# One explicit issue order for the set-up, two batches and the third attention of a fused attention and gated-MLP kernel

## The chip, the cores and the metric

The kernel runs on one core of a Trainium2 chip. Such a core has five engines, each with an instruction queue of its own: TensorE (PE in the rows; PEld is its weight load), VectorE (DVE), ScalarE (ACT), GpSimd (POOL) and SyncE (SP), which here only issues DMAs. They meet at semaphores. The metric is the device time of one execution in microseconds; lower is better.

## The reference, cut to what matters

Eight batches of 576 tokens with 512 channels (8 heads of 64). Packed attention: 32 pack queries per head attend over the keys and values, and the tokens then attend over the 32 packed rows. A gated convolution and a spatial gating MLP follow.

```python
p_packed = sm_attn(p, k, v)                 # softmax(scale * p k^T) v
x = sm_attn(q, p_packed, p_packed)          # heads side by side: 576 x 512
gate = sigmoid(sum_k conv_w[k] * shifted(x, k))     # 5 taps, causal
x = (gate * (x @ w_val)) @ w_out
h = relu(x @ w_in);  u, v = halves(h)
v_n = (v - mean(v)) / sqrt(var(v) + 1e-6)
out = (u * (w_spatial @ v_n + b_spatial)) @ w_out2
```

The weight matrices arrive as float64; the rest is float32.

## The kernel before, in words

**Precision.** Most products are made from a high and a low half of each operand, both in the `fp32r` type: `split` copies to the high half on ScalarE and subtracts on VectorE for the low half; `mm3` issues three matmuls for each product.

**Set-up.** A float64 block is turned into float32 by `from_f64` (a "unit"): one ScalarE activation (L460), three VectorE instructions (L464, L467, L468) and an addition (L471), on VectorE for the five blocks in `DADD` and on GpSimd for the rest. Units `uo`, `uw`, `uv`, `uu` are four blocks each of w_out, the v half of w_in, w_val and the u half of w_in; `wo` does the same with w_out2, then splits. Units `uu` and `wo` share one temporary buffer ("late"), the others have four. `fold` (`fv`, `fu`) multiplies w_out into w_in, and its result is split into `wp` (L506, L507). `spatial` (`ws`) loads and splits the spatial weights. `cw`, `cb`, `cx` make the first batch's gates by another way (convolution taps folded into the packed rows), with sigmoids on L299.

**A batch.** Attention of the next batch: `sa` (scores, row maxima, exponentials), `tr`, `av`, `ppt`, `sb` and `sb2` (second softmax), `m`, then `xt` (output transposed, in two halves; the second is followed by four channel convolutions, L307 to L314: a ScalarE copy into `acc`, four accumulating VectorE steps, a ScalarE sigmoid into `gate`). MLP of this batch: `val` (four tiles of 12 matmuls, multiplied by the gates on L337 and split into `g`), `hv` (five row tiles, normalised into `vn`), `hu`, `sp`, and `out` (four tiles of 24 matmuls, evacuated on L447, one output DMA each). A token's digit names the tile, head group or half.

**What sets the order.** `START` (set-up and first attention), `FIRST` (first batch's MLP with the rest of the set-up and the second attention) and `LOOP` (each later batch) are lists of tokens; `run` traces each token whole. A scheduler that works with a time model of its own then places the instructions of all tokens on the engines' queues and gives out the buffers; so a token's instructions are interleaved with those of its neighbours. Matmul results go through four PSUM buffers of two banks (pool `ps2`); `f` has eight buffers, `g` four, `kq` three.

Of the kernel before, what the change touches and what calls it, by code (L numbers as in the profile page):

```python
# [16 lines left out]
P = 128  # L17
UGB = 5
DADD = ('u2', 'o0', 'o1', 'w1', 'w0')
START = """  # L20
ik0 ip0 ro0 ic0 ik1 sa0 iv1 uo0 iv0 rw0 tr0 lv0 rv0 ro1 uo1 cw0 rv1 cb0 lk0 lq0 rw1 uw0 tr1 uo3 uw1 av0 uw2 uo2 uv0 av1 uv1 uw3 lq1 fv3 fv0 fv1 lk1 ppt0 sb0 sb20 sb21 fv2 uv3 uv2 lp0 m0 cx0 cx1 lv1
"""
FIRST = """
val1 ru1 val0 val3 ru0 lv0 val2 sa0 uu2 uu0 hv0 uu1 tr0 ws3 tr1 uu3 fu2 fu0 ws4 hv3 wo0 lv1 ws1 hv2 av0 av1 fu1 lq0 fu3 ppt0 lq1 wo1 hv1 hv4 ws0 sb0 hu1 hu2 ws2 sb20 lp0 hu3 sb21 hu0 wo3 lk0 lk1 sp0 sp2 sp1 wo2 sp3 m0 xt0 out1 xt1 out3 out0 out2
# [7 lines left out]
def packed_attention_gated_mlp(  # L32
# [72 lines left out]
    def load_kq(kind, b, g):  # L105
        src = kT if kind == "k" else qT
        t = kq_p.tile([P, 2, S], F32, tag="kq", name="kq")
        nc.sync.dma_start(out=t, in_=src[b, g])
        kq_t[kind, b, g] = t

    def load_v(b, g):
        t = v_p.tile([P, 4, 5, 65], F32, tag="v", name="v")
        nc.sync.dma_start(out=t, in_=vT[b, g])
        v_t[b, g] = t

    def load_p(b):
        t = sm_p.tile([P, NC * NPK], F32, tag="pbd", name="pbd")
        nc.sync.dma_start(out=t, in_=pT[b])
        pbd_t[b] = t

    class Attn:
        def __init__(self, b):
            self.b = b
            self.a, self.aT = {}, {}
            self.sT, self.A, self.an = {}, {}, {}
            self.gate = {}

# [8 lines left out]
        def sa(self, _):  # L136
            ps, heads = self.heads(pbd_t.pop(self.b), "k")
            for i in range(0, 8, 2):
                for qt in range(4):
                    for g, h, pT_, k in heads[i:i + 2]:  # L140
# [4 lines left out]
                        )  # L145
            mx = sm_p.tile([P, 8], F32, tag="mx", name="mx")
# [13 lines left out]
            for g in range(2):  # L160
                a = f_p.tile([P, S], F32, tag="f", name="a")
# [8 lines left out]
        def tr(self, g):  # L170
            aT = sm_p.tile([P, NB, NPK], F32, tag="aT", name="aT")
            nc.vector.transpose(out=aT.rearrange("p a b -> p (a b)"), in_=self.a.pop(g))
            self.aT[g] = aT

        def av(self, g):
# [12 lines left out]
            if g == 0:  # L188
# [13 lines left out]
        def ppt(self, _):  # L202
            ps = ps2.tile([P, 2, 512], F32, tag="ps2", name="ps2")[:, 0, :P]
            nc.tensor.transpose(ps, self.pp.rearrange("p a b -> p (a b)"), ident)
            self.ppT = pp_p.tile([P, P], F32, tag="ppT", name="ppT")
            nc.scalar.copy(out=self.ppT, in_=ps)

        def sb(self, _):
# [8 lines left out]
            for g in range(2):  # L217
                self.softmax_n(g, ps[g])

        def softmax_n(self, g, ps):  # L220
# [8 lines left out]
            )  # L229
            nc.scalar.activation(out=sTf, in_=sTf, func=AF.Exp, scale=scale)  # L230
            self.sT[g] = sT

        def sb2(self, g):
# [9 lines left out]
            nc.vector.transpose(out=an, in_=sT.rearrange("p a b -> p (a b)"))  # L243
            hi = am_p.tile([P, S], F32R, tag="Ah", name="Ah")
            lo = am_p.tile([P, S], F32R, tag="Al", name="Al")
            split(hi, lo, an)
            self.A[g] = (hi, lo)
            self.an[g] = an

        def m(self, _):  # L250
            ps = ps2.tile([P, 2, 512], F32, tag="ps2", name="ps2")
            for h in range(4):
                hs = slice(NPK * h, NPK * h + NPK)
                for g in range(2):
# [4 lines left out]
                    )  # L259
            hi = am_p.tile([P, 2, DM], F32R, tag="Mh", name="Mh", bufs=1)  # L260
            lo = am_p.tile([P, 2, DM], F32R, tag="Ml", name="Ml", bufs=1)
            split(hi, lo, ps)
            self.M = (hi, lo)

        def xt(self, n):
# [9 lines left out]
            if n == 0:  # L275
# [3 lines left out]
            if n == 1:  # L279
                for c in range(4):  # L280
                    self.conv(c, self.x[c // 2][:, c % 2, :])

        def cx(self, n):
            ps = [ps2.tile([P, 2, 512], F32, tag="ps2", name="ps2") for _ in range(2)]
            for tap in reversed(range(CONV)):
                sft = CONV - 1 - tap
                lo = sft if n == 0 else 0
                for h in range(4):
                    hs = slice(NPK * h, NPK * h + NPK)
                    for g in range(2):  # L290
# [12 lines left out]
        def conv(self, c, x):  # L303
# [3 lines left out]
            nc.scalar.activation(out=acc, in_=x, func=AF.Copy, scale=cw[:, c, CONV - 1:CONV])  # L307
            for tap in range(CONV - 1):
# [4 lines left out]
                )  # L313
            nc.scalar.activation(out=gt, in_=acc, func=AF.Sigmoid)  # L314

    class Mlp:
# [6 lines left out]
        def val(self, c):  # L323
# [3 lines left out]
            for n in range(2):  # L327
# [7 lines left out]
                )  # L335
            t = f_p.tile([P, S], F32, tag="f", name="g1")
            nc.vector.tensor_tensor(  # L337
                out=halves(t), in0=ps[:, :, :SH], in1=halves(at.gate.pop(c)), op=ALU.mult
            )
            g = g_p.tile([P, 2, S], F32R, tag="g", name="g")  # L340
            split(g[:, 0, :], g[:, 1, :], t)
            if not self.g1:
                self.tail = vr_p.tile([P, NC, P], F32R, tag="tail", name="tail", bufs=1)
            nc.vector.tensor_copy(
                self.tail[:, c, :].rearrange("p (a b) -> p a b", a=2), f32(g)[:, :, S - 64:]
            )
            self.g1[c] = g

        def hv(self, tt):
# [25 lines left out]
            nc.vector.tensor_scalar_add(rstd[:w], mv[:w, 1:2], 1e-6)  # L375
            nc.gpsimd.tensor_tensor(out=rstd[:w], in0=rstd[:w], in1=mhalf[:w], op=ALU.pow)  # L376
            nc.vector.tensor_scalar(  # L377
                out=vr[:w], in0=vr[:w], scalar1=mv[:w, 0:1], scalar2=rstd[:w],
                op0=ALU.subtract, op1=ALU.mult,
            )  # L380
            if tt < NT - 1:
                split(vn[0][:, tt, :], vn[1][:, tt, :], vr)
            else:
                split(vn[0][:64, tt, :], vn[0][64:, tt, :], vr[:w])
                nc.scalar.copy(out=vn[1][:64, tt, :], in_=vr[:w])

        def hu(self, c):
            ps = ps2.tile([P, 2, 512], F32, tag="ps2", name="ps2")
            cs = slice(P * c, P * c + P)
            for n in range(2):  # L390
# [10 lines left out]
                )  # L401
            u = ug_p.tile([P, S], F32, tag="ug", name="u")
            nc.scalar.activation(out=halves(u), in_=ps[:, :, :SH], func=AF.Relu)
            self.u[c] = u

        def sp(self, c):
            ps = ps2.tile([P, 2, 512], F32, tag="ps2", name="ps2")
            cs = slice(P * c, P * c + P)
            for n in range(2):
# [12 lines left out]
                )  # L422
            t = f_p.tile([P, S], F32, tag="f", name="g2")
            nc.vector.tensor_tensor(  # L424
                out=halves(t), in0=ps[:, :, :SH], in1=halves(self.u.pop(c)), op=ALU.mult
            )
            g = g_p.tile([P, 2, S], F32R, tag="g", name="g")
            split(g[:, 0, :], g[:, 1, :], t)
            self.g2[c] = g

        def out(self, e):
            ps = ps2.tile([P, 2, 512], F32, tag="ps2", name="ps2")
            cs = slice(P * e, P * e + P)
            for n in range(2):
# [21 lines left out]
    def from_f64(dst, raw, n, pool, tag, last=nc.gpsimd):  # L456
# [5 lines left out]
        )  # L462
        ci, ei = c.bitcast(I32), e.bitcast(I32)
# [6 lines left out]
        )  # L470
        last.tensor_tensor(out=dst, in0=dst, in1=c, op=ALU.add)  # L471

    def raw64(slot, srcs):
        n = len(srcs)
        raw = (vn_p if slot == "vn1" else const).tile([P, n, 512, 2], I32, tag=slot, name="raw")
        for i, src in enumerate(srcs):
            nc.sync.dma_start(out=raw[:, i], in_=words(src))
        return [raw[:, i] for i in range(n)]
# [5 lines left out]
    def load_raw(name, slot, w, lo):  # L484
        k0 = int(name[-1]) * 2
        got = raw64(slot, [w[:, k, lo:lo + DM] for k in (k0, k0 + 1)])
        for i in range(2):
            raws[name[:-1], k0 + i] = got[i]

    def unit(kind, k, dst, temps):  # L490
        from_f64(dst, raws.pop((kind, k)), DM, *temps, nc.vector if kind + str(k) in DADD else nc.gpsimd)
# [7 lines left out]
    def fold(m, hf):  # L499
# [4 lines left out]
        mms(ps, [(woT[k][:, cs], win[k]) for k in range(NC)])  # L504
        hi, lo = wp[0][:, m, hs], wp[1][:, m, hs]
        nc.scalar.copy(out=hi, in_=ps)  # L506
        nc.vector.tensor_tensor(out=lo, in0=ps, in1=f32(hi), op=ALU.subtract)  # L507

    def spatial(t):
        if not ws:  # L510
            ws[:] = [const.tile([P, NT, S], F32R, tag=f"ws{i}", name=f"ws{i}") for i in range(2)]
        st = f_p.tile([P, S], F32, tag="f", name="stage")
        if t < NT - 1:
            nc.sync.dma_start(out=st, in_=wsT[:, t, :])
            split(ws[0][:, t, :], ws[1][:, t, :], st)
            return
        nc.sync.dma_start(out=st, in_=wsT[:, t, :])
        nc.scalar.copy(out=ws[0][:, t, :], in_=st)
        st = f_p.tile([P, S], F32, tag="f", name="stage")
        nc.sync.dma_start(out=st[:97], in_=wsT[:97, t + 1, :])  # L520
        w = ws[1][:, t, :]
        nc.scalar.copy(out=w[64:96], in_=st[64:96])
        hi = f_p.tile([P, S], F32R, tag="f", name="hi")
        for r in (slice(0, 64), slice(96, 97)):
            split(hi[r], w[r], st[r])

    def final(k):
# [10 lines left out]
    def tap_rows():  # L538
# [6 lines left out]
        )  # L545
        ps = ps2.tile([P, 2, 512], F32, tag="ps2", name="ps2")
        nc.tensor.transpose(ps[:n, 1, P:2 * P], cw.rearrange("p a b -> p (a b)"), ident)
        t = sm_p.tile([n, P], F32, tag="cwt", name="cwt", bufs=1)
        nc.scalar.copy(out=t, in_=ps[:n, 1, P:2 * P])
        ps = ps2.tile([P, 2, 512], F32, tag="ps2", name="ps2").rearrange("p a b -> p (a b)")  # L550
        for k in range(CONV):
            nc.tensor.matmul(
                ps[:, P * k:P * k + P], lhsT=sel[:, k].rearrange("p a b -> p (a b)"), rhs=t, start=True, stop=True
            )
        r = x_p.tile([P, CONV, P], F32, tag="x", name="cwr")
        nc.scalar.copy(out=r.rearrange("p a b -> p (a b)"), in_=ps[:, :CONV * P])
        cwr.append(r)

    def run(order, b, at, ml):
        setup = {  # L560
# [113 lines left out]
```

## Time and profile before

| | us |
|---|---|
| three runs | 639.28, 638.68, 639.39 (median 639.28) |
| the profiled execution | 639.22 |
| its span, first to last instruction | 637.4 |
| PE busy in the span | 596.7 |
| DVE busy | 446.0 |
| ACT busy | 292.3 |
| POOL busy | 49.3 |

The span is one execution as the hardware profiler recorded it; 1.82 us of that execution lie outside it. Busy time is an average over a set-up and eight batches that are not alike, so the rows below go by stretch. A float32 matmul of an instruction list stands as two records in the trace, an `fp32r` one as one.

### The profile page before, as it was taken

To read this page: it belongs to the slowest core of one execution; us is meant where nothing else is said; L and a number is where in the kernel's file an instruction comes from. 1 tells how busy PE (TensorE), PEld (TensorE's weight loads), DVE (VectorE), ACT (ScalarE), POOL (GpSimd) and SP (SyncE) were. 2 spreads that over 40 slices of the span, in tenths; PEclk is the share of its full clock that TensorE was granted. 3 is DMA by queue.
4 is the path that set the end of the run, shared out by engine and by line. 5 is a ranking of instruction groups with operands and counts; after the bars stand their busy time and mean duration, and the time that the engine had idled before them with its cause. 6 is when DMAs were issued, how large, how long until landed. Compare 5 with 4: busy or idle time off the path is not lost.

```text
span 637.4 us, 12474 instructions
## 1 busy us (share of the span) xinstructions
PE 596.7 (94%) x5267; PEld 514.7 (81%) x5267; DVE 446.0 (70%) x873; ACT 292.3 (46%) x503; POOL 49.3 (8%) x67
## 2 busy tenths in 40 slices
PE   3687697999999999999999999999999999999997
PEld 2323663898988898899889888989889988989997
DVE  4998355977957696687759685869667875965640
ACT  2522435636463564346543655355533744363422
POOL 1242002200010000100010001000010001000100
PEclk9985797999999999999999999999999999999999
DMA  8960053302322012401222132202240110010001
GB/s 331 408 226 1 1 194 124 127 1 76 114 88 76 20 59 77 159 1 76 80 85 75 53 102 86 75 20 77 64 149 1 75 39 1 2 57 20 1 1 74
DMA packets 16569, 52.48 MB, mean 82 GB/s; under 512 B 1953, under 2 KB 2977, under 8 KB 16514
## 3 DMA queue, kind: packets, MB, share of 16 engines
q1 hardware_dynamic: 16514, 51.70, 22.7%
q8 instruction: 41, 0.67, 0.4%
q14 instruction: 14, 0.11, 0.1%
HBM read 42.25 MB, written 9.44 MB: 81 GB/s over the span
## 4 chain that ended last, share of the span: by engine, by line
PE 80%; DVE 9%; DMA 5%; ACT 3%; POOL 1%; issue 1%; SPq 0%; ACTq 0%; POOLq 0%
PE ps L95 72%; DMA raw<-w_outT 3%; DMA stage<-wsT 2%; PE ps L141 2%; DVE mx L148 2%; PE ps L271 1%; PE ps L181 1%; PE ps L212 1%; ACT L163 1%; DVE tmp L467 1%; PE ps L256 1%; ACT a L163 1%; DVE tmp L464 1%; DVE m L154 1%; POOL winu L471 1%
## 5 line engine op out<-in xcount | busy, mean ns | idle before, releaser
L95 PE MATMUL ps<-ws,vn 128*128 128x288 f32 (+1 forms) x896 | 124.0, 296 | 0.0
L95 PEld LDWEIGHTS ps<-ws,vn 128*128 128x128 f32 (+1 forms) x896 | 120.3, 188 | 2.9 <-issue 2.8
L95 PE MATMUL ps<-g,wp 128*128 128x288 f32 x768 | 113.6, 297 | 0.0
L95 PEld LDWEIGHTS ps<-g,wp 128*128 128x128 f32 x768 | 106.8, 188 | 4.4 <-DVE g L337 1.3
L95 PEld LDWEIGHTS ps<-g,wo 128*128 128x128 f32 x768 | 102.2, 188 | 6.1 <-issue 3.5
L95 PE MATMUL ps<-g,wo 128*128 128x288 f32 x768 | 105.6, 296 | 0.0
L95 PE MATMUL ps<-wp,g 128*128 128x512 f32 x384 | 98.7, 402 | 3.2 <-ACT a L163 3.2
L310 DVE SCALAR_TENSOR_TENSOR acc<-x,cw,acc 128x572 f32<-128x572 f32 (+3 forms) x112 | 82.6, 813 | 24.7 <-ACT acc L307 24.7
L95 PEld LDWEIGHTS ps<-wp,g 128*128 128x128 f32 x384 | 69.6, 188 | 22.1 <-ACT a L163 5.2
L90 ACT CAST g<-g 128x576 fp32r<-128x576 f32 x64 | 43.2, 674 | 73.7 <-DVE g L424 57.1
L376 POOL TENSOR_TENSOR rstd<-rstd,mhalf 128x1 f32<-128x1 f32 (+1 forms) x40 | 24.2, 606 | 460.7 <-DVE rstd L375 460.7
L91 DVE TENSOR_TENSOR g<-g,g 128x576 fp32r<-128x576 f32 x64 | 49.3, 772 | 11.0 <-ACT g L90 10.3
L371 DVE BATCH_NORM_STATS2 st<-vr 128x6 f32<-128x512 f32 (+1 forms) x40 | 27.5, 690 | 30.0 <-ACT vr L364 26.9
L95 PE MATMUL ps<-Ah,Mh 128*128 128x288 f32 x128 | 39.1, 305 | 5.1 <-ACT gate L299 5.1
L90 ACT CAST vn<-vr 128x512 fp32r<-128x512 f32 (+1 forms) x40 | 24.7, 618 | 33.5 <-DVE vr L377 33.5
L95 PE MATMUL ps<-Ah,Ml 128*128 128x288 f32 x128 | 39.0, 305 | 0.0
L95 PE MATMUL ps<-Al,Mh 128*128 128x288 f32 x128 | 39.0, 304 | 0.0
L424 DVE TENSOR_TENSOR g<-ps,u 128x576 f32<-128x576 f32 x32 | 24.1, 754 | 19.1 <-PE ps L95 19.0
L377 DVE TENSOR_SCALAR vr<-vr,mv,rstd 128x512 f32<-128x512 f32 (+1 forms) x40 | 21.5, 538 | 22.5 <-POOL rstd L376 22.4
L447 ACT COPY o<-ps 128x576 f32<-128x576 f32 x32 | 20.3, 635 | 34.8 <-PE ps L95 34.8
L91 DVE TENSOR_TENSOR vn<-vr,vn 128x512 fp32r<-128x512 f32 (+1 forms) x40 | 27.1, 680 | 11.4 <-ACT vn L90 11.3
L364 ACT ACTIVATE vr<-ps 128x512 f32<-128x512 f32 x32 | 19.5, 611 | 30.2 <-PE ps L95 17.4
(111 smaller groups left out, 735.8 us busy)
## 6 DMA issues: line engine op xcount, KB each, us to landing
v<-vT SPq DMA_DIRECT2D x16, 650.0 KB, 5.1
kq<-kT SPq DMA_DIRECT2D x16, 576.0 KB, 4.3
kq<-qT SPq DMA_DIRECT2D x16, 576.0 KB, 4.8
outT<-o SPq DMA_DIRECT2D x32, 288.0 KB, 2.1
raw<-w_in SPq DMA_DIRECT2D x8, 512.0 KB, 10.6
raw<-w_outT SPq DMA_DIRECT2D x4, 512.0 KB, 8.7
raw<-w_val SPq DMA_DIRECT2D x4, 512.0 KB, 9.4
raw<-w_out SPq DMA_DIRECT2D x4, 512.0 KB, 5.2
```

The lines of the kernel that those rows point to most:

```text
L90: nc.scalar.copy(out=hi, in_=src)
L91: nc.vector.tensor_tensor(out=lo, in0=src, in1=f32(hi), op=ALU.subtract)
L95: nc.tensor.matmul(out, lhsT=a, rhs=b, start=(i == 0), stop=(i == len(pairs) - 1))
L141: nc.tensor.matmul(ps[g][NPK * qt:NPK * qt + NPK, h // 2, SQ * (h % 2):SQ * (h % 2) + SQ], lhsT=pT_, rhs=k[:, SQ * qt:SQ * qt + SQ], start ...
L148: nc.vector.tensor_reduce(mx[:, 4 * g:4 * g + 4].rearrange("p (a b) -> p a b", a=2), ps[g][:, :, :SH].rearrange("p a (b c) -> p a b c", b= ...
L310: nc.vector.scalar_tensor_tensor(out=acc[:, sft:], in0=x[:, :S - sft], scalar=cw[:, c, tap:tap + 1], in1=acc[:, sft:], op0=ALU.mult, op1=A ...
L364: nc.scalar.activation(out=vr, in_=ps, func=AF.Relu)
L371: nc.vector.bn_stats(st[:w], vr[:w])
L376: nc.gpsimd.tensor_tensor(out=rstd[:w], in0=rstd[:w], in1=mhalf[:w], op=ALU.pow)
L377: nc.vector.tensor_scalar(out=vr[:w], in0=vr[:w], scalar1=mv[:w, 0:1], scalar2=rstd[:w], op0=ALU.subtract, op1=ALU.mult,)
L424: nc.vector.tensor_tensor(out=halves(t), in0=ps[:, :, :SH], in1=halves(self.u.pop(c)), op=ALU.mult)
L447: nc.scalar.copy(out=halves(t), in_=ps[:, :, :SH])
```

## The change

The token methods become generators with a `yield` between pieces: after the matmuls, between the ScalarE and the VectorE part of a split, before a DMA, and so on. `START` and `FIRST` and the first pass through `LOOP` are replaced by `HEAD`, a list of about 500 pieces: `tok` runs a token to its end, `tok.n` runs n of its pieces, and a leading digit is the batch. `HEAD` is traced inside `manual_schedule`, so that every engine gets its instructions in the order of the list. Batches 2 to 7 are traced with `LOOP` as before, by the scheduler. The instructions are the same ones on the same engines; two more loads of ScalarE's table are among them (18 in place of 16).

```diff
-START = """
-FIRST = """
+HEAD = """
+ro0.1 ip0 cb0.1 ro0 ik0 ik1 ro1 0ws3.1 ic0 uo0.1 lk0 uo0.1 rw0.1 uo1.1 iv1 uo0 uo1.1 iv0 sa0.1 uo1 rv0.1 uo2.1 sa0.1
...
+1xt1.2 1out3.1 1xt1.1 1out3 1xt1
 """
...
     def split(hi, lo, src):
         nc.scalar.copy(out=hi, in_=src)
+        yield
         nc.vector.tensor_tensor(out=lo, in0=src, in1=f32(hi), op=ALU.subtract)
...
             acc = f_p.tile([P, S], F32, tag="f", name="acc")
             nc.scalar.activation(out=acc, in_=x, func=AF.Copy, scale=cw[:, c, CONV - 1:CONV])
+            yield
             for tap in range(CONV - 1):
...
+            yield
             nc.scalar.activation(out=gt, in_=acc, func=AF.Sigmoid)
...
-    def run(order, b, at, ml):
...
+    def steps(b, name, i):
+        if name in setup:
+            return setup[name](i)
+        if name in load:
+            return load[name](b, i)
+        if hasattr(Mlp, name):
+            return getattr(mls[b], name)(i)
+        return getattr(ats[b + 1], name)(i) if b + 1 < B else ()
+
+    def run(order, batch):
+        live = {}
         for tok in order.split():
+            tok, _, n = tok.partition(".")
+            name = tok.lstrip("01")
+            b = batch if len(name) == len(tok) else int(tok[0])
+            if tok not in live:
+                live[tok] = steps(b, name[:-1], int(name[-1]))
+            for _ in itertools.islice(live[tok], int(n) if n else None):
+                pass
...
-    run(START, -1, at, None)
-    for b in range(B):
-        ml = Mlp(at)
-        at = Attn(b + 1) if b + 1 < B else None
-        run(FIRST if b == 0 else LOOP, b, at, ml)
+    with tc.manual_schedule():
+        run(HEAD, -1)
+    for b in range(2, B):
+        run(LOOP, b)
```

ScalarE's queue up to the first sigmoids, before. `raw_625` and `raw_584` are blocks of the u half of w_in, `raw_825` one of w_out2; `gate` is what the first batch's sigmoids write.

```order
L460 ACTIVATE tmp_715<-raw_625 128x512
L90 CAST Ah_428<-an_426 128x576
L460 ACTIVATE tmp_751<-raw_625 128x512
L460 ACTIVATE tmp_767<-raw_584 128x512
L460 ACTIVATE tmp_828<-raw_825 128x512
L299 ACT_TABLE_LOAD
L299 ACTIVATE gate_508<-ps2_466 128x288
```

The same place in the changed kernel. `raw_419` is a block of the u half of w_in, `Mh` the high half of the product that `val` multiplies with.

```order
L114 CAST Ah_466<-an_456 128x576
L342 ACT_TABLE_LOAD
L342 ACTIVATE gate_522<-ps2_471 128x288
L342 ACTIVATE gate_524<-ps2_471 128x288
L342 ACTIVATE gate_526<-ps2_472 128x288
L342 ACTIVATE gate_528<-ps2_472 128x288
L521 ACTIVATE tmp_545<-raw_419 128x512
L114 CAST Mh_589<-ps2_535 128x1024
```

Three unit activations moved from ahead of the first sigmoids to behind them, and the units of two blocks and of w_out2 behind `val`.

ScalarE's queue at the convolutions of the third batch's attention, before. `x` is the transposed attention output, two tiles of two channel groups; `acc` one group's accumulator; `o` an output tile of batch 1.

```order
L278 COPY x_2167<-ps2_2201 128x2x288
L307 ACTIVATE acc_2214<-x_2167,cw_103 128x576
L307 ACTIVATE acc_2222<-x_2167,cw_103 128x576
L278 COPY x_2168<-ps2_2202 128x2x288
L307 ACTIVATE acc_2230<-x_2168,cw_103 128x576
L307 ACTIVATE acc_2238<-x_2168,cw_103 128x576
L447 COPY o_2270<-ps2_2245 128x576
L447 COPY o_2298<-ps2_2273 128x576
L314 ACT_TABLE_LOAD
L314 ACTIVATE gate_2213<-acc_2214 128x576
L447 COPY o_2328<-ps2_2303 128x576
L314 ACTIVATE gate_2221<-acc_2222 128x576
```

The same place in the changed kernel.

```order
L319 COPY x_2168<-ps2_2258 128x2x288
L319 COPY x_2169<-ps2_2259 128x2x288
L350 ACTIVATE acc_2287<-x_2168,cw_103 128x576
L507 COPY o_2305<-ps2_2270 128x576
L359 ACT_TABLE_LOAD
L359 ACTIVATE gate_2286<-acc_2287 128x576
L350 ACTIVATE acc_2310<-x_2168,cw_103 128x576
L359 ACTIVATE gate_2309<-acc_2310 128x576
L350 ACTIVATE acc_2318<-x_2169,cw_103 128x576
L359 ACTIVATE gate_2317<-acc_2318 128x576
L350 ACTIVATE acc_2326<-x_2169,cw_103 128x576
```

Three of the four `acc` copies moved behind the sigmoid of the group before them.

TensorE's queue around the second half of `xt` (8 matmuls) of the same attention, before. The tile ahead of it is the first of batch 1's four `out` tiles; three more follow before the next batch's `val`.

```order
L95 MATMUL ps_2171<-g,wo_823 128x288 x2
L95 MATMUL ps_2171<-g,wo_824 128x288
L271 MATMUL ps_2201<-an,pp 64x288 x4
L271 MATMUL ps_2202<-an,pp 64x288 x4
L95 MATMUL ps_2245<-g,wo_823 128x288 x2
L95 MATMUL ps_2245<-g,wo_824 128x288
```

The same place in the changed kernel. The tile ahead of it is the third of the four `out` tiles; the tile behind it (`ps_2270`) is the last, and `val` follows at once.

```order
L120 MATMUL ps_2230<-g,wo_395 128x288 x2
L120 MATMUL ps_2230<-g,wo_396 128x288
L311 MATMUL ps_2258<-an,pp 64x288 x4
L311 MATMUL ps_2259<-an,pp 64x288 x4
L120 MATMUL ps_2270<-g,wo_395 128x288 x2
L120 MATMUL ps_2270<-g,wo_396 128x288
```

Two `out` tiles, 48 matmuls, moved from behind the second half of `xt` to ahead of it.

## Rows read from the trace of the kernel before

**Rows 1.** Page, busy tenths in 40 slices of the span; PEclk is the granted clock.

```profile
PE   3687697999999999999999999999999999999997
...
PEclk9985797999999999999999999999999999999999
```

**Rows 2.** Five stretches: busy us (instructions) by engine, granted clock, DMA share, GB/s.

```profile
0.00:70.26 70.26, 41.66 (x396) 19.89 (x396) 52.36 (x103) 23.76 (x45) 19.63 (x23) 0.87 0.57 219
70.26:118.19 47.93, 43.10 (x314) 29.56 (x314) 28.31 (x65) 21.94 (x45) 5.31 (x6) 0.87 0.31 106
118.19:220.45 102.26, 101.73 (x914) 92.69 (x914) 76.52 (x144) 49.25 (x82) 7.85 (x8) 1.00 0.22 75
220.45:245.50 25.05, 24.51 (x222) 22.89 (x221) 20.63 (x40) 14.93 (x25) 0.00 (x0) 1.00 0.28 97
245.50:637.40 391.90, 385.74 (x3425) 349.64 (x3425) 268.16 (x523) 182.44 (x309) 16.46 (x30) 1.00 0.16 56
```

**Rows 3.** Chain that ended last: start us, us, what.

```profile
66.23 1.27 POOL winu L471
...
67.53 0.66 ACT tmp L460
...
68.20 1.28 ACT L299
...
70.26 9.35 PE ps L95 x48
...
83.95 13.35 DMA stage<-wsT
...
117.03 1.16 PE ps L212 x32
...
216.41 3.37 PE ps L95 x24
...
239.78 1.42 DVE mx L148 x2
```

**Rows 4.** DVE in order of time: start, us, line, op, tiles [idle before, releaser].

```profile
12.44 1.42 DVE L148 TENSOR_REDUCE mx<-ps 128x4 f32<-128x576 f32 x2
...
24.49 0.69 DVE L471 TENSOR_TENSOR winv<-winv,tmp 128x512 f32<-128x512 f32 x1
...
29.75 1.37 DVE L467 TENSOR_SCALAR tmp<-tmp 128x512 int32<-128x512 int32 x1
...
37.40 0.75 DVE L226 TENSOR_REDUCE mx<-sT 128x18 f32<-128x576 f32 x1
38.19 0.76 DVE L227 TENSOR_TENSOR sT<-sT,mx 128x576 f32<-128x576 f32 x1
...
58.48 0.75 DVE L91 TENSOR_TENSOR Al<-an,Ah 128x576 fp32r<-128x576 f32 x1
...
61.55 0.43 DVE L467 TENSOR_SCALAR tmp<-tmp 128x512 int32<-128x512 int32 x1
...
221.98 11.00 DVE L310 SCALAR_TENSOR_TENSOR acc<-x,cw,acc 128x572 f32<-128x572 f32 x15 [3.58 <-ACT acc L307]
```

**Rows 5.** POOL in order of time, one addition of the set-up.

```profile
29.45 1.38 POOL L471 TENSOR_TENSOR woT<-woT,tmp 128x512 f32<-128x512 f32 x1 [0.96 <-DVE woT L468]
```

**Rows 6.** PE in order of time, first `val` matmul and the one wait behind it.

```profile
70.26 0.61 PE L95 MATMUL ps<-Ah,Mh 128*128 128x288 f32 x1 [5.05 <-ACT gate L299]
...
102.02 1.31 PE L181 MATMUL ps<-v,aT 128*32 128x65 f32 x40 [4.21 <-DVE wp L507]
```

**Rows 7.** ACT in order of time around the spatial weights and the convolutions.

```profile
97.37 0.67 ACT L522 CAST ws<-stage 32x576 fp32r<-32x576 f32 x1 [7.56 <-DMA stage<-wsT]
...
220.49 0.64 ACT L278 COPY x<-ps 128x576 f32<-128x576 f32 x1
221.17 1.45 ACT L307 ACTIVATE acc<-x,cw 128x576 f32<-128x576 f32 x2
...
229.37 0.69 ACT L314 ACTIVATE gate<-acc 128x576 f32<-128x576 f32 x1 [0.38 <-DVE acc L310]
```

More of the change, by code (lines that the diff above doesn't have):

```diff
@@ L1 @@
+import itertools
 from contextlib import ExitStack
@@ L119, in load_p @@
         pbd_t[b] = t
+        yield
     class Attn:
@@ L217, in sb @@
             for g in range(2):
-                self.softmax_n(g, ps[g])
+                yield
+                yield from self.softmax_n(g, ps[g])
         def softmax_n(self, g, ps):
@@ L243, in sb2 @@
             nc.vector.transpose(out=an, in_=sT.rearrange("p a b -> p (a b)"))
+            self.an[g] = an
+            yield
             hi = am_p.tile([P, S], F32R, tag="Ah", name="Ah")
             lo = am_p.tile([P, S], F32R, tag="Al", name="Al")
-            split(hi, lo, an)
             self.A[g] = (hi, lo)
-            self.an[g] = an
+            yield from split(hi, lo, an)
         def m(self, _):
@@ L259, in m @@
                     )
+            yield
             hi = am_p.tile([P, 2, DM], F32R, tag="Mh", name="Mh", bufs=1)
             lo = am_p.tile([P, 2, DM], F32R, tag="Ml", name="Ml", bufs=1)
-            split(hi, lo, ps)
             self.M = (hi, lo)
+            yield from split(hi, lo, ps)
         def xt(self, n):
@@ L280, in xt @@
                 for c in range(4):
-                    self.conv(c, self.x[c // 2][:, c % 2, :])
+                    yield
+                    yield from self.conv(c, self.x[c // 2][:, c % 2, :])
         def cx(self, n):
@@ L339, in val @@
             )
+            yield
             g = g_p.tile([P, 2, S], F32R, tag="g", name="g")
-            split(g[:, 0, :], g[:, 1, :], t)
             if not self.g1:
                 self.tail = vr_p.tile([P, NC, P], F32R, tag="tail", name="tail", bufs=1)
+            self.g1[c] = g
+            yield from split(g[:, 0, :], g[:, 1, :], t)
             nc.vector.tensor_copy(
@@ L380, in hv @@
             )
+            yield
             if tt < NT - 1:
-                split(vn[0][:, tt, :], vn[1][:, tt, :], vr)
+                yield from split(vn[0][:, tt, :], vn[1][:, tt, :], vr)
             else:
-                split(vn[0][:64, tt, :], vn[0][64:, tt, :], vr[:w])
+                yield from split(vn[0][:64, tt, :], vn[0][64:, tt, :], vr[:w])
+                yield
                 nc.scalar.copy(out=vn[1][:64, tt, :], in_=vr[:w])
@@ L426, in sp @@
             )
+            yield
             g = g_p.tile([P, 2, S], F32R, tag="g", name="g")
-            split(g[:, 0, :], g[:, 1, :], t)
             self.g2[c] = g
+            yield from split(g[:, 0, :], g[:, 1, :], t)
         def out(self, e):
@@ L470, in from_f64 @@
         )
+        yield
         last.tensor_tensor(out=dst, in0=dst, in1=c, op=ALU.add)
[L473 to L478, printed above, removed]
     woT, winv, winu = [], [], []
@@ L485, in load_raw @@
         k0 = int(name[-1]) * 2
-        got = raw64(slot, [w[:, k, lo:lo + DM] for k in (k0, k0 + 1)])
+        raw = (vn_p if slot == "vn1" else const).tile([P, 2, 512, 2], I32, tag=slot, name="raw")
         for i in range(2):
-            raws[name[:-1], k0 + i] = got[i]
+            if i:
+                yield
+            nc.sync.dma_start(out=raw[:, i], in_=words(w[:, k0 + i, lo:lo + DM]))
+            raws[name[:-1], k0 + i] = raw[:, i]
     def unit(kind, k, dst, temps):
-        from_f64(dst, raws.pop((kind, k)), DM, *temps, nc.vector if kind + str(k) in DADD else nc.gpsimd)
+        return from_f64(dst, raws.pop((kind, k)), DM, *temps, nc.vector if kind + str(k) in DADD else nc.gpsimd)
     def u_half(k):
@@ L503, in fold @@
         hs = slice(hf * DM, (hf + 1) * DM)
-        mms(ps, [(woT[k][:, cs], win[k]) for k in range(NC)])
+        for k in range(NC):
+            nc.tensor.matmul(ps, lhsT=woT[k][:, cs], rhs=win[k], start=(k == 0), stop=(k == NC - 1))
+            yield
         hi, lo = wp[0][:, m, hs], wp[1][:, m, hs]
         nc.scalar.copy(out=hi, in_=ps)
+        yield
         nc.vector.tensor_tensor(out=lo, in0=ps, in1=f32(hi), op=ALU.subtract)
@@ L512, in spatial @@
         st = f_p.tile([P, S], F32, tag="f", name="stage")
+        nc.sync.dma_start(out=st, in_=wsT[:, t, :])
+        yield
         if t < NT - 1:
-            nc.sync.dma_start(out=st, in_=wsT[:, t, :])
-            split(ws[0][:, t, :], ws[1][:, t, :], st)
+            yield from split(ws[0][:, t, :], ws[1][:, t, :], st)
             return
-        nc.sync.dma_start(out=st, in_=wsT[:, t, :])
         nc.scalar.copy(out=ws[0][:, t, :], in_=st)
+        yield
         st = f_p.tile([P, S], F32, tag="f", name="stage")
         nc.sync.dma_start(out=st[:97], in_=wsT[:97, t + 1, :])
+        yield
         w = ws[1][:, t, :]
@@ L524, in spatial @@
         for r in (slice(0, 64), slice(96, 97)):
-            split(hi[r], w[r], st[r])
+            yield from split(hi[r], w[r], st[r])
+            yield
     def final(k):
@@ L531, in final @@
         nc.sync.dma_start(out=raw, in_=words(w_out2[:, k, :]))
+        yield
         t = f_p.tile([P, S], F32, tag="f", name="stage")[:, :DM]
-        from_f64(t, raw, DM, *late)
-        split(wo2[0][:, k, :], wo2[1][:, k, :], t)
+        yield from from_f64(t, raw, DM, *late)
+        yield
+        yield from split(wo2[0][:, k, :], wo2[1][:, k, :], t)
     cwr = []
@@ L597, in packed_attention_gated_mlp, with load_cw @@
-    at = Attn(0)
+    def load_cw():
+        nc.sync.dma_start(out=cw64, in_=words(conv_w))
+        yield
+    ats = [Attn(b) for b in range(B)]
+    mls = [Mlp(at) for at in ats]
+    setup = {
+        "cw": lambda i: from_f64(cw.rearrange("p a b -> p (a b)"), cw64, NC * CONV, *early),
+        "cb": lambda i: tap_rows(),
+        "ro": lambda i: load_raw(f"o{i}", ("wo20", "ws1")[i], w_outT, 0),
+        "rw": lambda i: load_raw(f"w{i}", ("wo21", "vn1")[i], w_in, DM),
+        "rv": lambda i: load_raw(f"v{i}", ("wo20", "wo21")[i], w_val, 0),
+        "ru": lambda i: load_raw(f"u{i}", ("ws1", "wo20")[i], w_in, 0),
+        "uo": lambda k: unit("o", k, woT[k], early),
+        "uw": lambda k: unit("w", k, winv[k], early),
+        "uv": lambda k: unit("v", k, wval[:, k, :], early),
+        "uu": lambda k: unit("u", k, u_half(k), late),
+        "fv": lambda m: fold(m, 1),
+        "fu": lambda m: fold(m, 0),
+        "ws": spatial,
+        "wo": final,
+        "ip": load_p,
+        "ik": lambda i: load_kq("k", 0, i),
+        "iv": lambda i: load_v(0, i),
+        "ic": lambda i: load_cw(),
+    }
```

116 lines of the change are left out of this document (69 added, 47 removed).

## The prediction, made before the changed kernel ran

> **What bounds the kernel now.** I read the page's slices first: TensorE is at nine tenths from the eighth slice on, and below that, at a granted clock down to half, only before [rows 1]. So there are two regimes. The stretches say how much each holds [rows 2]: from 245.50 us to the end TensorE works 385.74 of 391.90 us; from 118.19 to 245.50 it lacks about 1 us. All the idle time worth having is ahead of 118.19 us: 70.26 - 41.66 = 28.60 us before the first `val`, 47.93 - 43.10 = 4.83 us between it and the first `hu`.
>
> Then the chain, to see what ends those waits. The first `val` starts at 70.26 us because ScalarE's sigmoids came late, and they came late because their queue held unit activations, each waiting for GpSimd to give back the one "late" buffer: POOL addition, activation, table load, sigmoid, matmul [rows 3]; the matmul had waited 5.05 us [rows 6]. Ahead of that VectorE works almost without a gap from the row maxima at 12.44 to the last low half `Al`, which ends at 59.23 us [rows 4]. So the set-up has two limits in series: some 46.8 us of VectorE, then 11.0 us of sigmoids kept back. Between `val` and `hu` it is a DMA of the spatial weights, 13.35 us on the chain [rows 3], for which ScalarE waited 7.56 us [rows 7]; TensorE felt 4.21 us of it [rows 6].
>
> I cut the execution at four marks on TensorE: V (first `val`, 70.26), H (first `hu`, 118.19), X (the third attention's second `xt` half done, 220.45) and Y (245.50, where TensorE resumes behind the next attention's exponentials). Behind Y the two versions have the same 2898 matmuls in the same order, so 391.90 us stay. The new value of each stretch follows.
>
> **V, 57.5 us.** The instructions that VectorE has in its queue from the row maxima to `Ml`, the last operand of `val`, are those of before up to `Al`, less one unit addition and one `wp` subtraction (0.6 us each at the pitch of the rows, durations 0.69 in [rows 4]) and with `cw` added (0.3): -0.9 us. A VectorE instruction that meets a GpSimd addition lasts longer: L467 took 1.37 us beside an addition of 1.38 us and 0.43 us alone [rows 4, 5], 0.94 us for each meeting. Before, seven such meetings lie ahead of 59 us; in the new order I count six, since transposes or PSUM reads follow some units. So 12.44 + 46.79 - 0.9 - 0.9 = 57.4, taken as 57.5. TensorE's four folds, two `cx` and `m` fit beside it. Of the moved unit activations one still waits for the late buffer, but ahead of `Ml` and not of the sigmoids of the first half. Bounds: no meeting costs anything (seven times 0.94 less: 51.7), or nothing is gained but the sigmoids' 11 us and some transposes wait too (61).
>
> The Trainium skill (SBUF — State Buffer, Who interferes with whom) says that VectorE and GpSimd share a pair of ports under an exclusive lock, and that a VectorE instruction with at most one SBUF input, outside the fast modes, doesn't take it. The 1.37 us agree with the lock; no row here shows a transpose beside a GpSimd addition. By the rule the transposes put behind units hide an addition each; without it V would be about 2 us later.
>
> **V to H, 43.6 us.** Work stays: 43.10 us, less `sb` (1.16) [rows 3], which now follows H: 41.9. The spatial weights are loaded before 50 us and split late, so the 4.83 us of idle time go. In their place I see two short waits: the third block of the u half of w_in is finished only as the first `fu` fold wants it, and `hu` waits for the split of the last fold (ScalarE 0.6, VectorE 0.7). I put 1.7 us; 0 to 8 are possible, since VectorE now has some 36 us of work in these 43, by a count of its queue at the durations before.
>
> **H to X, 111.4 us.** Before 102.26. The 0.53 us idle go, `sb` comes in (1.16), and two `out` tiles of 24 matmuls move ahead of X: 2 x 3.37 = 6.74 [rows 3]. That is 109.6. Walking the queues I find short waits only (`hv` for the last `g`, a PSUM buffer behind a ScalarE copy): 1.8 us, 0 to 5. On SP the load of a key tile waits from about 138 us for `sb` of the third attention at about 185, and batch 0's output DMAs stand behind it; the buffers that they hold are wanted again only after that, so I put nothing.
>
> **X to Y, 31.0 us.** Here the cost is. Before, four `acc` copies were made at once and VectorE ran 15 convolution steps in 11.00 us, alternating groups, 0.73 us each [rows 4, 7]. Now each group's copy stands on ScalarE behind the sigmoid of the group before, so the two engines take turns. The four steps of a group also depend on each other, and a VectorE instruction that depends on the one before starts only after its whole duration (0.75 us long, next one 0.79 later [rows 4]), so a group takes about 4 x 0.85 = 3.4 us. From X: two `x` copies and `acc` (0.64, 0.61, 0.75) to 2.1; three rounds of 3.4 + sigmoid 0.69 + copy 0.75 to 16.4; meanwhile the first three `val` products; the fourth group between splits of `g` to 22.5; its sigmoid, product, split to 25.2; then from the maxima to TensorE's release, 245.50 - 239.78 = 5.72 [rows 3]: 30.9, with a gap or two 31.0. TensorE reaches `val` 6.74 us earlier than before, so it only waits longer: it has 18.3 us of work in 31.0. Bounds: not under 25.05 (the same VectorE work as before), not over 34.
>
> The Trainium skill (ScalarE: Activation LUTs, What ACT_TABLE_LOAD costs) gives 2.66 us for each change of table, with a drain behind the load. The trace disagrees: the load of 1.28 us at 68.20 is followed by a sigmoid at 69.50 [rows 3]. By the rule the load in this chain would end 1.4 us later and Y with it; by the trace it is inside the sum.
>
> **Sum.** 57.5 + 43.6 + 111.4 + 31.0 + 391.9 = 635.4 us of span, against 637.4; with 1.82 us outside, 637.2 us, where the profiled execution took 639.22 and the median is 639.28. About 17 us are won ahead of the first `hu`, and 15 are given back: 9 between H and X and 6 behind X. The 6.74 us of `out` are not lost as work, but as cover: they no longer stand beside the convolutions.
>
> **Rivals.**
> *The convolutions run as tightly as before* (X to Y 25.05): 637.2 - 5.95 = 631.3 us. For it: the VectorE work is the same. Against: the queue order of ScalarE, in which a copy can't pass a sigmoid. It would need `val` to be late enough to hide the turns.
> *The set-up gains more.* The 48 matmuls of the first `val` took 9.35 us, 0.195 each, where `out` matmuls of the same shape took 3.37 / 24 = 0.14 [rows 3], behind TensorE's idle time and at a granted clock of 0.87 in that stretch [rows 2]; if the denser folds and `cx` leave the clock higher, some 2.6 us go, and with half of the meetings hidden, 3 us more: 631.6 us. Against: TensorE still waits before V.
> *Slower: VectorE becomes the bound between `val` and the folds.* Place: the first `hv` to the split of the last fold. `hv` tiles, the units of `wo` and `uu`, maxima and transposes stand in one fixed queue, and each normalisation waits for GpSimd. Four additions block for 0.94 us each, 3.8 us, and one wait for a load like that of before costs TensorE 4.2 [rows 6]: 8.0 us instead of 1.7, or 643.5 us. It decides from about 3.5 us of waits on. For it: 36 us of VectorE in 43. Against: TensorE has four PSUM buffers to run ahead with.
>
> **How the numbers follow.** Forecast 637.2 us, with its own range of 634 to 641: chance 0.46. Convolutions tight 0.2, set-up better 0.14, VectorE bound 0.2. A difference below 0.2% (1.3 us) can't be told from none. The forecast lies 0.8 us beyond that border, so about half of its weight is faster, a third within, the rest slower; the two middle rivals are faster nearly whole, the last is slower. That gives 0.56 faster, 0.18 the same, 0.26 slower. The range goes from 629 us (both gains, in part) to 645 us.
>
> **What would show it.** Right: the first `val` at 56 to 59 us, released by VectorE's `Ml` and not by a sigmoid; the first `hu` near 101; the third attention's second `xt` half done near 212.5; then TensorE idle for some 12 us before the next `hv`, with ScalarE and VectorE taking turns on the convolutions. Wrong: `val` still released by sigmoids or before 54 us; waits for VectorE adding to over 4 us before `hu`; a wait of under 8 us behind X; or any difference behind Y.

## The result, and the profile after

The changed kernel takes 646.98 us (median of 4 runs, 645.01 to 648.14), the kernel before 638.98 (4 runs, 637.57 to 639.39): 1.0126 times as long, 95% interval 1.0093 to 1.0159. The forecast was 637.2 us with 645 as the upper end of its range. In the profiled execution (645.01 us, the shortest of the four; span 643.1) the four marks V, H, X and Y lie at 57.90, 96.12, 219.10 and 251.34 us:

| stretch | before | forecast | after |
|---|---|---|---|
| to V | 70.26 | 57.5 | 57.90 |
| V to H | 47.93 | 43.6 | 38.22 |
| H to X | 102.26 | 111.4 | 122.98 |
| X to Y | 25.05 | 31.0 | 32.24 |
| Y to the end | 391.90 | 391.9 | 391.76 |

Forecast and measured span differ by 643.1 - 635.4 = 7.7 us: +0.4, -5.4, +11.6, +1.2 and -0.1. So one stretch holds the whole error, and another hides half of it.

The page's slices of the changed kernel, as [rows 1], each slice 16.1 us:

```profile
PE   1688994999999949999999999999999999999997
...
PEclk9999997999999967999999999999999999999999
```

The climb to nine tenths comes earlier than before, and the clock is at nine tenths from the start. New is the seventh slice, where TensorE falls to 4 and its granted clock to 7; the fifteenth (225 to 241 us) is the forecast wait behind the convolutions. The stretches, as [rows 2], with H to X cut in three around the hole (columns: from:to, length, busy us and instructions on PE, PEld, DVE, ACT, POOL, then granted clock, DMA share, GB/s):

```profile
0.00:57.90 57.90, 33.80 (x396) 16.59 (x397) 47.52 (x94) 23.74 (x47) 15.40 (x19) 1.00 0.75 291
57.90:96.12 38.22, 37.21 (x281) 24.81 (x281) 33.59 (x74) 20.30 (x39) 11.43 (x13) 1.00 0.29 94
96.12:102.50 6.38, 6.31 (x75) 5.43 (x69) 4.98 (x10) 3.33 (x7) 0.00 (x0) 1.00 0.37 117
102.50:111.88 9.38, 0.00 (x1) 0.00 (x1) 0.57 (x1) 1.91 (x4) 0.00 (x0) 0.61 0.39 136
111.88:219.10 107.22, 105.61 (x926) 94.80 (x926) 74.82 (x135) 48.81 (x80) 4.58 (x6) 0.99 0.17 58
219.10:251.34 32.24, 22.46 (x172) 18.72 (x173) 21.50 (x40) 13.42 (x22) 0.00 (x0) 0.74 0.17 57
251.34:643.10 391.76, 385.74 (x3425) 349.64 (x3425) 268.19 (x523) 182.47 (x309) 16.48 (x30) 1.00 0.16 56
```

From 102.50 to 111.88 us TensorE does nothing. TensorE in order of time (idle time and its releaser in brackets, as [rows 6]) shows the wait that V had before shrunk from 5.05 to 1.99 us and released by `Ml`, as forecast, and then a wait that no step of the prediction has:

```profile
57.90 0.40 PE L120 MATMUL ps<-Ah,Mh 128*128 128x288 f32 x1 [1.99 <-DVE Ml L116]
...
111.88 1.96 PE L295 MATMUL ps<-wval,ppT 64*32 64x512 f32 x16 [9.45 <-ACT u L461]
```

ScalarE in order of time, where [rows 7] stood before, tells why `u` was late:

```profile
99.74 0.27 ACT L242 COPY ppT<-ps 128x128 f32<-128x128 f32 x1 [0.56 <-PE ps L239]
109.92 0.67 ACT L586 CAST ws<-stage 32x576 fp32r<-32x576 f32 x1 [9.91 <-DMA stage<-wsT]
110.61 0.67 ACT L114 CAST hi<-stage 64x576 fp32r<-64x576 f32 x1
111.19 0.64 ACT L461 ACTIVATE u<-ps 128x576 f32<-128x576 f32 x1
```

The queue is in order: `u`, whose matmuls were long done, stands behind two copies of the last piece of the spatial weights, and these wait for its load. `u` frees the PSUM buffer that the product `m` (L295) needs. The chain, as [rows 3], puts the load's whole flight on the path; it is issued (L583) behind a `v` load (L139) that waits for `av` (L213):

```profile
95.48 0.76 PE ps L213 x40
...
96.25 0.33 SPq L139
...
96.68 13.21 DMA stage<-wsT
...
109.92 0.68 ACT ws L586
...
110.61 0.67 ACT hi L114
111.28 0.55 ACT u L461
```

Before, the same load took 13.35 us on the chain [rows 3]. Its duration is nearly the same in both kernels; what changed is who stands behind it.

Why 13.2 us for 218.2 KB? The DMA view from 96 to 112 us (40 slices of 0.4 us, then issues with KB each and median us to landing):

```profile
GB/s 0 0 13 234 169 260 429 390 181 6 17 23 70 23 29 23 29 23 156 196 363 397 366 293 311 365 294 79 23 29 23 29 23 23 35 23 23 31 41 31
...
v<-vT SPq DMA_DIRECT2D x1, 650.0 KB, 3.9
kq<-kT SPq DMA_DIRECT2D x1, 576.0 KB, 8.8
raw<-w_out SPq DMA_DIRECT2D x1, 512.0 KB, 9.6
stage<-wsT SPq DMA_DIRECT2D x1, 218.2 KB
```

While other loads run, up to 429 GB/s flow; when only the stage load is left, some 23. In such a stretch, 108.00 to 109.40 us, the mean busy share of the 16 DMA engines (the column ahead of GB/s) is 0.06, one sixteenth:

```profile
108.00:109.40 1.40, 0.00 (x0) 0.00 (x0) 0.00 (x0) 0.00 (x0) 0.00 (x0) 0.50 0.06 25
```

In the trace its 97 packets of 2304 bytes run from 99.48 to 109.44 us, one starting every 0.09 us: no more than one engine carries them at a time. The piece has 97 rows. The Trainium skill (DMA: Bandwidth & Descriptors, Why a DMA increments its semaphore by 16 and not by 1) says that a transfer is spread over as many of the 16 DMA engines as the largest number up to 16 that divides its row count, and lists 127 rows as going to one engine. 97 is prime too. That the row count is the reason is a theory to be tried; its rivals are the late issue and the bandwidth shared with `kq` and `raw`.

### The profile page after: what moved, and what is told of

Same layout as the page of the kernel before. It is cut to its first block, busy times and chain, and to the rows that moved or that the text cites. A ratio compares the mean times of both kernels' runs of the same rounds, so it can differ in the third digit from the quotient of the medians.

```text
span 643.1 us, 12469 instructions
## 1 busy us (share of the span) xinstructions
PE 591.1 (92%) x5267; PEld 510.0 (79%) x5267; DVE 451.2 (70%) x873; ACT 294.0 (46%) x505; POOL 47.9 (7%) x67
## 4 chain that ended last, share of the span: by engine, by line
PE 72%; DVE 17%; ACT 5%; DMA 3%; issue 1%; POOL 0%; SPq 0%; ACTq 0%; DVEq 0%; POOLq 0%
PE ps L120 63%; DVE acc L354 3%; PE ps L564 2%; DMA stage<-wsT 2%; DVE g L116 2%; PE ps L311 2%; DVE tmp L529 2%; DVE mx L178 2%; PE ps L170 1%; PE ps L295 1%; PE ps L213 1%; DMA kq<-kT 1%; PE ps L248 1%; ACT L194 1%; DVE g L383 1%
## 5 line engine op out<-in xcount | busy, mean ns | idle before, releaser
L120 PE MATMUL ps<-g,wp 128*128 128x288 f32 x768 | 115.7, 301 | 9.1 <-ACT g L114 9.1
L120 PEld LDWEIGHTS ps<-g,wp 128*128 128x128 f32 x768 | 108.1, 190 | 16.2 <-ACT g L114 9.4
L354 DVE SCALAR_TENSOR_TENSOR acc<-x,cw,acc 128x572 f32<-128x572 f32 (+3 forms) x112 | 85.1, 813 | 34.1 <-ACT acc L350 33.3
L429 POOL TENSOR_TENSOR rstd<-rstd,mhalf 128x1 f32<-128x1 f32 (+1 forms) x40 | 22.9, 575 | 478.0 <-DVE rstd L427 474.2
L116 DVE TENSOR_TENSOR g<-g,g 128x576 fp32r<-128x576 f32 x64 | 47.9, 753 | 13.0 <-ACT g L114 12.5
L461 ACT ACTIVATE u<-ps 128x576 f32<-128x576 f32 x32 | 20.9, 654 | 27.4 <-PE ps L120 27.4
```

The source lines that it names most:

```text
L120: nc.tensor.matmul(out, lhsT=a, rhs=b, start=(i == 0), stop=(i == len(pairs) - 1))
L354: nc.vector.scalar_tensor_tensor(out=acc[:, sft:], in0=x[:, :S - sft], scalar=cw[:, c, tap:tap + 1], in1=acc[:, sft:], op0=ALU.mult, op1=A ...
```

## The experiments

**1. Changed kernel, 98 rows.** 98 = 7 x 14, and the array has zeros there.

```diff
-        nc.sync.dma_start(out=st[:97], in_=wsT[:97, t + 1, :])
+        nc.sync.dma_start(out=st[:98], in_=wsT[:98, t + 1, :])
```

> The changed kernel, with the second piece of the last spatial weights loaded as 98 rows instead of 97 (the row more is zeros and is not used). Theory A, the row count: a load of 97 rows, which no number from 2 to 16 divides, is carried by one of the 16 transfer engines and so lands 13.2 us after its issue; 98 rows go over 14 of them and land within 3 to 6 us although they are 1% more bytes. ACT's wait of 9.91 us falls to 0 to 2, TensorE's of 9.45 us at the third mixing product likewise, and the time falls by 7 to 10 us, to 637 to 640. Theory B, the late issue and the shared bandwidth: 1% more bytes at the same moment beside the same two loads land after 13 us again, and the time stays within 1 us.

Measured: 635.26 us (6 runs), ratio to the kernel before 0.9945 (0.9925 to 0.9965). The chain's row and ScalarE's, in order of time:

```profile
96.55 3.86 DMA stage<-wsT
```

```profile
99.60 0.27 ACT L242 COPY ppT<-ps 128x128 f32<-128x128 f32 x1 [0.55 <-PE ps L239]
100.43 0.67 ACT L586 CAST ws<-stage 32x576 fp32r<-32x576 f32 x1 [0.57 <-DMA stage<-wsT]
101.13 0.67 ACT L114 CAST hi<-stage 64x576 fp32r<-64x576 f32 x1
101.71 0.64 ACT L461 ACTIVATE u<-ps 128x576 f32<-128x576 f32 x1
```

TensorE's product `m` follows at once, without a wait:

```profile
102.40 1.09 PE L295 MATMUL ps<-wval,ppT 64*32 64x512 f32 x16
```

One row more, the same place in every queue, and the load lands in 3.86 us; its 98 packets run from 98.79 to 99.95 us. Theory B falls. The gain, 11.7 us between the medians, is larger than I expected. TensorE's stretch from `m` to X shows a part of it: 106.04 us at a granted clock of 1.00 against 107.22 at 0.99 behind the idle time.

**2. Kernel before, 98 rows.** The same edit; every engine has the same instructions in the same order.

> The kernel before, with the same load as 98 rows; no instruction changes its place. Theory A: the load lands 3 to 6 us after its issue at 70.6 instead of 13.35 us, so ACT's wait of 7.56 us goes, TensorE's of 4.21 us at 102 with it or in part, and the time falls by 2 to 5 us, to 634 to 637. Theory B: the load shares with the three others issued beside it, lands as late as before, and the time stays within 0.7 us.

Measured: 632.16 us (6 runs), ratio 0.9888 (0.9869 to 0.9907). The load is issued at 83.95 us in the kernel before [rows 3]; the 70.6 of the expectation is a slip. ScalarE's wait of 7.56 us [rows 7] becomes 0.16 us, and TensorE's of 4.21 [rows 6] is gone:

```profile
89.73 0.67 ACT L522 CAST ws<-stage 32x576 fp32r<-32x576 f32 x1 [0.16 <-DMA stage<-wsT]
```

```profile
96.78 1.36 PE L181 MATMUL ps<-v,aT 128*32 128x65 f32 x80
```

So the load cost the kernel before some 6.3 us (638.44 - 632.16), 2 more than the one wait: V to H fell from 47.93 to 40.3 us. TensorE's idle time in it fell from 4.83 to 0.63 us, and its busy time, for the same 314 records, from 43.10 to 39.64 at a granted clock of 0.95 instead of 0.87. The gain passed my upper bound of 5 for that reason.

**3. Changed kernel, 97 rows, the copies later in ScalarE's order.** The diff shows two places of one line of `HEAD`; its other tokens are left out.

```diff
-0wo0 0ws4.1 0sb0.1 0hu0 0ws4.2 0m0.1
+0wo0 0sb0.1 0hu0 0m0.1
...
-0wo2.1 0hu2.1 0m0.1 0ws4 0hu3.1 0hu2 0m0 0sb0.1 0sb20.1 0sp2.1
+0wo2.1 0hu2.1 0m0.1 0hu3.1 0hu2 0m0 0sb0.1 0ws4 0sb20.1 0sp2.1
```

> The changed kernel, with the load left at 97 rows and its three ACT copies moved in ACT's order from in front of the u activation of the first hidden block to behind the second one and the mixing product's split, just ahead of the first spatial product. Theory A1, the cost was ACT's order: the load still lands 13 us after its issue, but nobody waits for it for longer than 1 or 2 us, TensorE's wait of 9.45 us goes, and the time falls by 6 to 10 us, to 637 to 641. Rival: the landing itself is what is late, the wait reappears at the first spatial product or at an ACT copy behind the new place, and the time falls by 0 to 4 us only.

Measured: 641.71 us (9 runs), 5.3 us under the first result. The outcome lies between the two: TensorE's wait of 9.45 us is gone, and half of it comes back where the weights are needed:

```profile
112.77 3.46 PE L120 MATMUL ps<-ws,vn 97*128 97x288 f32 x13 [4.54 <-DVE ws L116]
```

So the order of the queue made the load cost 9.45 us instead of 4.54, and the load's 13 us are too long for either place.

**4. Changed kernel, 97 rows, convolution interleaved.** For the third attention: four starts, then each tap over the four channels, then four gates, which is the order of the kernel before.

```diff
+            if n == 1 and self.b == 2:
+                yield
+                convs = [self.conv(c, self.x[c // 2][:, c % 2, :]) for c in range(4)]
+                for step in range(CONV):
+                    for co in convs:
+                        next(co)
...
```

> The changed kernel, with the third attention's convolution issued as the kernel before had it: four ACT starts first, then the 16 DVE steps tap by tap over the four channels, then the four gates. Theory: the stretch from the end of the third attention's second half to TensorE's restart falls from 32.2 us to 24 to 27 (16 steps of 0.73 us instead of 0.85, and no ACT and DVE taking turns), so the time falls by 5 to 8 us, to 639 to 642. Rival: TensorE is held by the next softmax alone, and the gates that now all come at the end make the gated products wait as long; the time falls by 0 to 2 us.

Measured: 640.42 us (12 runs), 6.6 us under the first result. VectorE in order of time, in the changed kernel and then in this one:

```profile
221.01 3.37 DVE L354 SCALAR_TENSOR_TENSOR acc<-x,cw,acc 128x572 f32<-128x572 f32 x4 [9.47 <-ACT acc L350]
227.13 3.37 DVE L354 SCALAR_TENSOR_TENSOR acc<-x,cw,acc 128x572 f32<-128x572 f32 x4 [2.76 <-ACT acc L350]
231.97 3.37 DVE L354 SCALAR_TENSOR_TENSOR acc<-x,cw,acc 128x572 f32<-128x572 f32 x4 [1.47 <-ACT acc L350]
```

```profile
222.41 11.71 DVE L364 SCALAR_TENSOR_TENSOR acc<-x,cw,acc 128x572 f32<-128x572 f32 x16 [9.47 <-ACT acc L360]
```

Twelve steps in three rounds with waits take 14.3 us there, sixteen take 11.7 here, as in [rows 4]. From X to the end it is 419.4 us instead of 424.0: 4.6 in the trace. So the prediction's term for the turns of ScalarE and VectorE was real, and this much of it is the order. The medians differ by 2 us more than these stretches; with 98 rows (run 7) medians and stretches both give some 5.

**5. The changed kernel again.**

> The changed kernel once more, unaltered, beside the others of this call, because its four first runs reached from 645.0 to 648.1 us while the kernel before stayed within 2. If those four stand for it, the median is 645 to 648 and the first result holds; if they were taken in a bad hour, it is 642 to 644 and the gains measured against it so far (11.7 us for the 98 rows, 6.6 for the convolution) are 3 to 4 us too large.

Measured: 647.87 us (4 runs, 647.65 to 648.07), ratio 1.0134 (1.0112 to 1.0156). The first result holds. By the stretches it is longer than the first by 0.7 us from V to H (granted clock 0.96 there), by 0.4 from H to X and by 1.5 behind Y. Its trace has a wait of 2.0 us for the exponentials behind Y, in batches that the change doesn't touch, which the first trace lacks. It is about as large as the distance between the lower and the upper of the first four runs; what brings it stays open.

**6. Changed kernel, 101 rows.** Prime again, with 4% more bytes.

> The changed kernel with 101 rows in the load instead of 97 (more rows of zeros). Theory A, the row count's divisors: 101 has none from 2 to 16 either, so one transfer engine carries it, it lands 13.5 to 14 us after its issue (101/97 of 13.2 is 13.75), and the time is that of the changed kernel or up to 1 us more. Rival, 97 is the odd case out (a partition limit at 96, or the piece behind the 96th row): 101 rows behave as 98 did, land within 4 us, and the time is about 635.

Measured: 647.99 us (4 runs), the time of run 5. The chain, in order of time:

```profile
97.00 13.30 DMA stage<-wsT
```

97 and 101 rows land after 13.2 and 13.3 us, 98 after 3.9. Neither the bytes nor the rows past the 96th decide. The traces agree with the rule of the Trainium skill named above. The packet counts fit it too: from 96 to 113 us both traces hold three loads of 128 rows and this one; the packets under 512 B are 49 with 97 rows and then 62 with 98:

```profile
DMA packets 532, 2.03 MB, mean 119 GB/s; under 512 B 49, under 2 KB 49, under 8 KB 530
```

```profile
DMA packets 546, 2.03 MB, mean 119 GB/s; under 512 B 62, under 2 KB 62, under 8 KB 544
```

Sixteen for each of the three others and 1 or 14 for this one would give just these: 48 + 1 and 48 + 14. An odd row count that has a divisor, as 99 = 9 x 11, was not run, so by the times alone the rival "odd counts are slow" still stands; the 14 speaks against it.

**7. 98 rows and the interleaved convolution.**

> The changed kernel with both edits, 98 rows and the third attention's convolution interleaved as in the kernel before. Theory: the two lie in different stretches (103 to 110 us and 219 to 251 us) and add: 635.3 less 5 to 7 is 628 to 631, under both kernels and under the kernel before with 98 rows (632.2). Rival: the wait behind the convolution is set by the next softmax, whose keys and maxima come no earlier, so the second edit brings 0 to 2 here: 633 to 635.

Measured: 630.20 us (4 runs), ratio 0.9858 (0.9839 to 0.9876). The two gains add: 635.26 - 630.20 = 5.1 us here, and 423.96 against 419.31 us from X to the end in the traces.

**8. As 7, with the third attention's second half ahead of the third output tile.** The diff shows the ends of two lines of `HEAD`.

```diff
-1out1.1 1out0 1out2.1 1out1 1out2.1 1xt1.1 1out2.1 1out3.1 1out2
-1xt1.2 1out3.1 1xt1.1 1out3 1xt1
+1out1.1 1out0 1xt1.1 1out1 1out2.1 1xt1.2 1out2.1 1xt1.1 1out2.1 1out3.1 1out2
+1out3.1 1out3 1xt1
```

> As the run before, and the third attention's second half set ahead of the third output tile on TensorE, with its x copies and convolution starts ahead of that tile's copy on ACT. Theory: 24 matmuls more (3.4 us) lie beside the convolution, so TensorE waits 2 to 4 us less: 625 to 628. Rival: the gates wait for DVE, which ends only as much earlier as it starts, and the table loads of the sigmoid on ACT are unmoved; what TensorE gains before, it waits longer behind: 0 to 1 us.

Measured: 627.07 us (4 runs, 626.43 to 628.43), ratio 0.9810 (0.9789 to 0.9832). TensorE's wait behind the convolution in the changed kernel, in run 7 and in run 8:

```profile
237.97 0.61 PE L120 MATMUL ps<-g,wp 128*128 128x288 f32 x1 [9.14 <-ACT g L114]
```

```profile
225.78 0.61 PE L120 MATMUL ps<-g,wp 128*128 128x288 f32 x1 [6.67 <-ACT g L114]
```

```profile
222.32 0.61 PE L120 MATMUL ps<-g,wp 128*128 128x288 f32 x1 [3.49 <-ACT g L114]
```

The 3.2 us between the last two are the 24 matmuls that now stand beside the convolution: in both runs 15.3 us lie between ScalarE's first `acc` copy and this matmul (210.46 to 225.78 and 207.01 to 222.32 us). This version beats both kernels; what it still waits for here is 3.49 us.

Medians of all versions:

| version | 97 rows | 98 rows |
|---|---|---|
| before | 638.4 to 639.7 | 632.2 |
| changed | 647.0, 647.9 | 635.3 |
| changed, convolution interleaved | 640.4 | 630.2 |
| and second half earlier | not run | 627.1 |

## Why the prediction was wrong

**To V: right in kind, and its number in part by luck.** The first `val` starts at 57.90 us, released by `Ml` and not by a sigmoid, in the forecast's 56 to 59. But three terms of the sum were off and nearly cancel: the row maxima start at 11.37 us instead of 12.44, five VectorE instructions instead of six meet a GpSimd addition, at 0.94 us each, and the moved unit that waits for the late buffer, which the sum put at nothing, holds VectorE for 2.14 us ahead of `Ml`:

```profile
55.22 0.43 DVE L526 TENSOR_SCALAR tmp<-tmp 128x512 int32<-128x512 int32 x1 [2.14 <-ACT tmp L521]
```

**V to H: the step that failed, and a term mis-sized besides.** The step is the sentence "The spatial weights are loaded before 50 us and split late, so the 4.83 us of idle time go." That holds for the first pieces only. The second piece of the last tile is loaded at 96.68 us, behind a `v` load on SP, and the chain of before had shown its 13.35 us [rows 3]. I read them as a load among others that loses its cost with its place; they belong to the load itself (runs 1, 2 and 6). In the walk through the queues of **H to X** ("short waits only ... 1.8 us, 0 to 5") this load was therefore taken as landed: waits were 9.45 + 1.33 + 0.22 = 11.0 us. With 98 rows H to X is 112.5 us (208.44 - 95.98), against 111.4 forecast, and the whole 635.26, against 637.2.

The rest of V to H was mis-sized to the other side. I carried over 43.10 us of work from a stretch with a granted clock of 0.87; the new stretch runs at 1.00 with 37.21 us busy. 41.9 x 0.87 = 36.5 would have been close. Run 2 shows the same on one and the same order of instructions: 43.10 us at 0.87 and 39.64 at 0.95. The rival "set-up better" named this for 48 matmuls only.

**X to Y: right in kind, 1.2 us short.** The turns of ScalarE and VectorE are in the trace, at 3.37 us a round as worked out. What is missing is a load of ScalarE's table. Two lie in this stretch; the one for the exponentials, at 248.80 us, is inside the 5.72 us from the maxima to TensorE, but the one ahead of the first sigmoid has no term in the sum:

```profile
224.45 1.28 ACT L359 ACT_TABLE_LOAD   x1 [1.32 <-DVE acc L354]
```

The rounds (2.1 us of copies, then three times 3.4 + 0.69 + 0.75, which is 16.6 and not 16.4) leave it out. It makes VectorE's first wait between rounds 2.76 us where the next is 1.47. The sigmoid starts at 225.75, 0.02 us behind the load. TensorE's wait is 9.14 us instead of some 12, because its work in this stretch takes 22.46 us at a granted clock of 0.74, where 18.3 were counted. That doesn't move Y: run 5 has 19.88 us of work there at 0.84, in the same 32.25 us.

**The rivals.** The slower one put 8.0 us of waits between the first `hv` and the last fold and laid them on VectorE. The wait that came is of that size, but lies behind the first `hu` and belongs to a load; its aside on "one wait for a load like that of before" had the right cause and priced it at TensorE's 4.2 us instead of the 13 us of flight.

**What the change itself is worth.** With the load mended on both sides, the new order takes 635.26 us against 632.16, so it loses some 3 us; with the convolution's order of before it takes 630.20 and wins 2 (the intervals just touch). Between the traces of the two with 98 rows, the time up to H falls from 111.08 to 95.98 us, by 15.1, where 17 were forecast; H to X grows by 10.1 (102.32 to 112.46) and X to Y by 7.2 (25.04 to 32.25), where 9 and 6 were forecast. The convolution's order is 5 of what is given back.

## What to carry to other kernels

A long load on the chain has to be explained before its cost is moved or dropped: set its bytes against the rate of the slices in which it runs alone, and ask what stands behind its consumer in the new order. Give a load a row count with a large divisor up to 16, and pad it where the array has the rows. A work term carried from a stretch with a lowered granted clock is to be rescaled where the idle time ahead of it goes.

## What the runs showed of the hardware

A load on one DMA engine also delays those issued behind it: in the changed kernel the `kq` and `raw` loads that follow land after 8.8 and 9.6 us (listed above), with 98 rows after 4.1 and 4.9. The same DMA view of run 1, from 96 to 112 us:

```profile
GB/s 0 0 104 286 273 325 409 382 323 127 0 0 41 0 20 0 0 0 173 115 334 334 367 330 435 420 225 51 0 0 0 0 0 0 0 0 0 0 0 0
...
kq<-kT SPq DMA_DIRECT2D x1, 576.0 KB, 4.1
raw<-w_out SPq DMA_DIRECT2D x1, 512.0 KB, 4.9
```

The tail of some 23 GB/s is gone. And in the 9.4 us without a matmul TensorE's granted clock is 0.61, where it was 1.00 (2.4 GHz) in the stretch before. It is at 0.50 (1.2 GHz) when the product `m` starts, whose 16 matmuls take 1.96 us, against 1.09 in run 1:

```profile
111.88:113.00 1.12, 1.12 (x16) 0.23 (x16) 1.08 (x4) 0.64 (x1) 0.00 (x0) 0.50 0.01 4
```
